# Attention backward on one core: constant matmuls in all four half-steps, the key burst in one, a longer offset, a second value buffer

## Chip, cores, metric

One core of a Trainium2 chip. The metric is the device time of one launch in microseconds (us). Engines: PE (matmul), PEld (its weight loads), DVE (vector), ACT (scalar), POOL (GpSimd), SP (issues most transfers).

## The reference

A gated mix of a 32-head attention block and an S4 convolution, with the gradients of all twelve differentiable inputs. What matters here is attention, forward and backward, for 2048 tokens, 576 channels, heads of 18:

```python
scores = jnp.einsum("bhqd,bhkd->bhqk", q, k) * (Dh ** -0.5)
p = _softmax(scores, axis=-1)
o = jnp.einsum("bhqk,bhkd->bhqd", p, v)
...
_out, _vjp = jax.vjp(_f, A_x, A_wqkv, A_wo, ...)
_grads = _vjp(grad_out)
```

## The kernel before

Heads go in 8 groups of four, 32 rows of the array each; a *unit* is one group with one quarter of the queries (512). A loop over *half-steps* G runs a unit's forward part and, OFF half-steps later, the backward part of an earlier unit. A half-step issues six score rows (32 x 512, of three kinds), then one or two *bursts* that use all 128 rows and 32 columns for each head, then the exps on ACT and the products on DVE. Four half-steps, 16 exps, I call a *quad*; a unit is eight quads. A score row uses 32 rows and 128 columns of the array, a burst's matmuls 128 rows and 32 columns each; going from one shape to the other is a change of *tiling mode*, and the wait that it costs a *drain*.

```python
for nm, src, nb in (("QaT", QaT_d[g], 2), ("KaT", KaT_d[g], 2), ("VaT", VaT_d[g], 1)):
    T[nm] = ga.tile([P, S], BF, tag=nm, bufs=nb, name=nm + "_g")
    nc.sync.dma_start(T[nm], src)
for nm, src, nb in (("Vtok", VaT_d[g], 2), ("Ktok", KaT_d[g], 1), ("Qtok", QaT_d[g], 1)):
    T[nm] = ga.tile([P, NT, 4, HP], BF, tag=nm, bufs=nb, name=nm + "_g")
    nc.sync.dma_start_transpose(out=T[nm].rearrange("p t h w -> p t (h w)"), in_=src)
# ... cut ...
def row(kind, g, b, l, r, j):            # score rows: 4 buffers "S", 2 buffers "dP"
    tg, nb = ("dP", 2) if kind == "P2" else ("S", 4)
    ps = apsp.tile([P, KB], F32, tag=tg, bufs=nb, name="ps_" + kind)
    mm(ps, lhsT=l[r0:r0 + DA], rhs=r[r0:r0 + DA], tile_position=(r0, 0))
# ... cut: in half-step G, G2 = G - OFF, after the six rows ...
if G % 4 == 1 and G2 >= 4:           evs.append(dv_burst(...))      # value burst
if G % 4 == 2 and G2 >= 5:           evs.append(dq_burst(...))      # query burst
if G % 4 in (3, 0) and G2 >= 10:     e_ = dk_half(...)              # key burst, one half each
if G % 4 in (3, 0) and G >= 3:       mm(accO ...)                   # output burst, forward
for (kind, g, b, i, j, ps) in rows:  # ACT: exp of P1 (PT) and P3 (eb); DVE: ds = ps * PT
    ...
for e_ in evs: e_()                  # DVE adds each burst's bank "accB" (one bank) to SBUF
```

PE, ACT, DVE and POOL run in program order; SP's transfers are ordered by the framework's scheduler.

## Time and profile before

| | before |
|---|---|
| median of three runs | 3932.82 us (3932.32 to 3941.81) |
| first exp to last forward exp | 252.1 to 2458.5 us |
| PE, ACT, DVE busy, of the span | 77, 72, 75% |
| mean granted clock, 334 to 2458 us | 0.65 |

The prediction reads the stage in stretches of four microseconds and shows those lines.

### The profile page before, as it was taken

Reading aid. Unit: us, or ns where it says so; the run is one execution under the profiler, and the core shown is the slowest. Engines: PE = TensorE matmul, PEld = TensorE weight load, DVE = VectorE, ACT = ScalarE, POOL = GpSimd, SP = SyncE. Lnnn points to the kernel's source line nnn. Section 1 sums busy time; section 2 is a strip of 40 time slices with the busy share of each in tenths; the row PEclk is TensorE's granted clock in tenths of the full one; section 3 lists DMA queues with packets and bytes.
Section 4 is the critical chain, followed back from the end, with each engine's and each line's share of the span. In section 5 each row is a group of like instructions: output and inputs, shape, how many; then the busy total and the mean of one; then the engine's idle time right before and its main releaser. Section 6 shows DMA issues by size and latency. Waiting matters only on the chain. (4 is left out here: it accounts for less than half of the span.)

```text
span 3930.1 us, 64060 instructions
## 1 busy us (share of the span) xinstructions
PE 3008.7 (77%) x24020; PEld 1073.6 (27%) x24020; DVE 2944.3 (75%) x5131; ACT 2842.5 (72%) x5253; POOL 63.2 (2%) x147
## 2 busy tenths in 40 slices
PE   7969999989999999999999999779344554445421
PEld 2312222222222222222222222135233333333320
DVE  5618878878878878878878878625288888888867
ACT  4549999999989999999999999500266666666610
POOL 0000000000000000000000000100000000000000
PEclk9955666666657666666666666588555555555555
DMA  8535587685686786686776776876456656555456
GB/s 197 166 89 126 128 161 143 133 165 133 138 158 132 138 161 132 138 163 134 142 159 130 135 150 128 184 213 150 69 96 110 110 109 114 103 101 102 85 146 193
DMA packets 1860137, 536.78 MB, mean 137 GB/s; under 512 B 1774991, under 2 KB 1838553, under 8 KB 1859826
## 3 DMA queue, kind: packets, MB, share of 16 engines
q1 hardware_dynamic: 1859826, 532.69, 64.6%
q8 instruction: 189, 3.10, 0.3%
q14 instruction: 122, 1.00, 0.1%
HBM read 99.74 MB, written 60.96 MB: 41 GB/s over the span
## 5 line engine op out<-in xcount | busy, mean ns | idle before, releaser
L602 DVE TENSOR_TENSOR ds<-ps_P,PT 128x512 bf16<-128x512 f32 x2048 | 1360.0, 687 | 353.1 <-PE ps_P L30 226.5
L593 ACT ACTIVATE PT<-ps_P 128x512 bf16<-128x512 f32 x2048 | 1325.6, 652 | 133.6 <-PE ps_P L30 123.3
L597 ACT ACTIVATE eb<-ps_P 128x512 bf16<-128x512 f32 x2048 | 1343.2, 658 | 21.5 <-PE ps_P L30 21.3
L30 PE MATMUL ps_P<-dOaT,VaT_g 32*128 32x512 bf16 x2048 | 1033.6, 530 | 46.9 <-DMA VaT_g<-VaT_d 34.8
L30 PE MATMUL ps_P<-KaT_g,QaT_g 32*128 32x512 bf16 x2048 | 993.4, 520 | 43.9 <-ACT PT L593 4.6
L30 PE MATMUL ps_P<-QaT_g,KaT_g 32*128 32x512 bf16 x2048 | 948.2, 534 | 38.6 <-DMA KaT_g<-KaT_d 6.0
L30 PEld LDWEIGHTS <-KaT_g 32*128 32x128 bf16 x2048 | 150.4, 101 | 647.2 <-issue 632.2
L30 PEld LDWEIGHTS <-VaT_g 32*128 32x128 bf16 x2048 | 192.5, 96 | 419.0 <-issue 373.7
L30 PE MATMUL accO<-PT,Vtok_g 128*32 128x512 bf16 x2048 | 299.9, 568 | 0.0
L30 PE MATMUL accK<-dsT,Qtok_g 128*32 128x256 bf16 x4096 | 285.5, 371 | 5.7 <-DVE dqa L479 3.5
L30 PE MATMUL accQ<-ds,Ktok_g 128*32 128x512 bf16 x2048 | 234.5, 550 | 1.2 <-DVE dvacc L462 0.8
L30 PE MATMUL accV<-eb,dOa 128*32 128x512 bf16 x2048 | 230.3, 541 | 0.6 <-DVE dkacc L503 0.6
L30 PEld LDWEIGHTS <-QaT_g 32*128 32x128 bf16 x2048 | 173.5, 97 | 192.0 <-issue 180.0
L30 PE MATMUL uvp<-RX,E1e 128*128 128x64 bf16 x1152 | 134.2, 290 | 107.8 <-DVE E1e L901 107.8
L30 PE MATMUL tps<-RX,T0w 128*128 128x32 bf16 x576 | 38.4, 233 | 215.5 <-DVE yd L1036 190.5
L882 ACT ACTIVATE kk<-ph,magc 128x512 f32<-128x512 f32 x144 | 91.1, 686 | 147.4 <-DVE E1e L900 112.7
L30 PE MATMUL ph<-thr,lrow 3*128 3x512 bf16 x288 | 124.6, 562 | 88.4 <-ACT ab L875 60.2
L462 DVE TENSOR_TENSOR dvacc<-dvacc,accV 128x512 f32<-128x512 f32 x224 | 153.3, 684 | 26.6 <-PE accV L30 22.3
L479 DVE TENSOR_TENSOR dqa<-dqa,accQ 128x512 f32<-128x512 f32 x224 | 153.1, 684 | 25.1 <-PE accQ L30 22.2
L30 PEld LDWEIGHTS <-E1e 128*128 128x128 bf16 x1152 | 125.3, 124 | 128.9 <-DVE E1e L901 128.3
L30 PE MATMUL ybp<-Rw,E1n 128*128 128x31 bf16 x1152 | 70.0, 233 | 104.2 <-ACT ydi L973 101.5
L887 DVE SCALAR_TENSOR_TENSOR kk<-kk,ph 128x512 f32<-128x512 f32 x144 | 95.1, 682 | 71.6 <-ACT kk L882 71.6
(267 smaller groups left out, 3337.0 us busy)
## 6 DMA issues: line engine op xcount, KB each, us to landing
T0w<-Kp_d SPq DMA_DIRECT2D x36, 512.0 KB
dsT<-ds SPq DMA_TRANSPOSE x512
dqkv_d<-dtk SPq DMA_DIRECT2D x96, 72.0 KB
dqkv_tok<-dqkv_d SPq DMA_DIRECT2D x1, 6912.0 KB
Md_d<-mst SPq DMA_DIRECT2D x144, 36.0 KB
ga_d<-ga_st SPq DMA_DIRECT2D x16, 288.0 KB
dxm_d<-dxm SPq DMA_DIRECT2D x16, 288.0 KB
skw<-Md_d SPq DMA_DIRECT2D x72, 64.0 KB
```

The source lines that it names most:

```text
L30: return nc.tensor.matmul(out, lhsT=lhsT, rhs=rhs, start=start, stop=stop, **kw)
L462: nc.vector.tensor_tensor(a_, a_, acc, op=A.add)
L479: nc.vector.tensor_tensor(U["dqa"], U["dqa"], acc, op=A.add)
L593: nc.scalar.activation(U["PT"][i][:, j, :], ps, ACT.Exp)
L597: nc.scalar.activation(e, ps, ACT.Exp)
L602: nc.vector.tensor_tensor(U["ds"][i][:, j, :], ps, U["PT"][i][:, j, :], op=A.mult)
L882: nc.scalar.activation(B_["kk"][h][:, 4 * q:4 * q + 4, :], ph, ACT.Identity, bias=magc, scale=1.0)
L887: nc.vector.scalar_tensor_tensor(v_, v_, MAGIC, B_["ph"].pop((h, q)), op0=A.subtract, op1=A.subtract)
```

## The change

It adds seven matmuls a quad of an exchange matrix with an identity, whose results nobody reads, to keep the array's clock up; gathers the key burst in one half-step and moves the output bursts to the value and query half-steps, so that one half-step is free for four constants; lengthens the offset by two half-steps (from 37 to 39); gives the value tile a second buffer; and splits the DVE work on a finished unit. Small tiles lose buffers to make room. NFILL holds the number of constants in the value, query, key and empty half-step; the runs below are named by it (const_0004). A constant uses the whole array, a third tiling mode.

```diff
+            NFILL = (1, 1, 1, 4)
-                ptp = ctx.enter_context(tc.tile_pool(name="ptp", bufs=20))
+                ptp = ctx.enter_context(tc.tile_pool(name="ptp", bufs=21))
-                    for nm, src, nb in (... ("VaT", VaT_d[g], 1)):
+                    for nm, src, nb in (... ("VaT", VaT_d[g], 2)):
-                OFF = NST + 5
+                OFF = NST + 7
+                def fill(acc, n, w=4):
+                    o_ = acc[:, (4 - w) * P:4 * P].rearrange("p (a b) -> p a b", b=P)
+                    for _ in range(n):
+                        mm(o_, lhsT=J_bf, rhs=fill_r[:, 0:w, :])
 ... the output burst comes first, then:
+                    if ph in (0, 1, 2):
+                        ACC.append(accB(("accV", "accQ", "accK")[ph]))
+                        fill(ACC[0], NFILL[ph])
+                    elif 0 <= G2 < NTOT:
+                        fill(accB("accF"), NFILL[3])
 ... then value burst (G2 % 4 == 0), query burst (1), whole key burst (2)
 ... post_forward: product, sum and negation of dO move from f1 to f2, one half-step later
 ... one buffer for oT, rl, Ob, dl, dqa; dOa 3 -> 2; eb 12 -> 10
```

## The prediction

> **What bounds the kernel now.** I read the page's busy row and its slices first, then stretches of the attention stage (the only stage the change touches), then two timelines, then the waits.
>
> ```profile
> PE 3008.7 (77%) x24020; PEld 1073.6 (27%) x24020; DVE 2944.3 (75%) x5131; ACT 2842.5 (72%) x5253; POOL 63.2 (2%) x147
> ...
> PE   7969999989999999999999999779344554445421
> ...
> ACT  4549999999989999999999999500266666666610
> ...
> PEclk9955666666657666666666666588555555555555
> ```
>
> Slices 4 to 25 are attention: PE and ACT both read 9, and the granted clock reads only 0.5 to 0.7. A PE that looks full at a low clock may be full only because of it. In stretches of four microseconds:
>
> ```profile
> 412.00:416.00 4.00, 3.56 (x31) 1.07 (x30) 3.67 (x7) 4.00 (x9) 0.00 (x0) 1.00 0.58 131
> 416.00:420.00 4.00, 3.78 (x36) 1.16 (x34) 3.05 (x6) 3.97 (x9) 0.00 (x0) 0.65 0.59 133
> ...
> 476.00:480.00 4.00, 4.00 (x33) 0.86 (x25) 3.05 (x6) 3.76 (x8) 0.00 (x0) 0.50 0.58 131
> 480.00:484.00 4.00, 4.00 (x35) 1.00 (x32) 3.30 (x6) 3.77 (x9) 0.00 (x0) 0.50 0.55 125
> ```
>
> (Columns: stretch, length, busy PE, weight loads, DVE, ACT, POOL, clock, DMA share, GB/s.) At clock 1.00 ACT is busy 4.00 of 4.00 and PE has room. At 0.50 PE is busy 4.00 of 4.00 and ACT is not. The clock alternates, mean 0.65 from 334 to 2458 us. The exps show the pace in the two states, first at full clock, then at half:
>
> ```profile
> 412.75 0.69 ACT L593 ACTIVATE PT<-ps_P 128x512 bf16<-128x512 f32 x1
> 413.23 0.70 ACT L597 ACTIVATE eb<-ps_P 128x512 bf16<-128x512 f32 x1
> 413.70 0.71 ACT L593 ACTIVATE PT<-ps_P 128x512 bf16<-128x512 f32 x1
> ```
>
> ```profile
> 2152.21 0.60 ACT L593 ACTIVATE PT<-ps_P 128x512 bf16<-128x512 f32 x1
> 2152.69 0.62 ACT L597 ACTIVATE eb<-ps_P 128x512 bf16<-128x512 f32 x1
> 2153.38 0.60 ACT L593 ACTIVATE PT<-ps_P 128x512 bf16<-128x512 f32 x1
> ```
>
> At full clock one exp starts every 0.477 us without a break, though a record lasts 0.7 us (records overlap, so starts are counted, not lengths). At half clock each fourth exp comes 0.69 us after the third: it waited for a score row. I call four half-steps a quad: 16 exps. ACT-bound it takes 16 x 0.477 = 7.63 us; at half clock the exps from 2150.55 to 2154.82 give 4.27 us for two half-steps, 8.53 a quad. The waits name one more thing:
>
> ```profile
> ACT PT L593 <- PE ps_P L30: 118.8, 239, 5.7
> ...
> PE ps_P L30 <- DMA VaT_g<-VaT_d: 34.8, 7, 5.7
> ```
>
> Seven group changes, 5 us each, wait for the value tile, which has one buffer.
>
> **What the Trainium skill says.** (1) "TensorE: Matmul & The Clock Gate", Part 1: an activity monitor gives the array half or full clock and decides on free-running windows of about 3.4 us. The trace agrees: in this stage the clock is only 0.5 or 1.0, and changes at multiples of 3.4 us. The page speaks of how busy PE is; here PE is busy 4.00 of 4.00 at clock 0.50 for up to 37.5 us, so busy by records can't be the measure. (2) The same page, "Back-to-back issue gap": N/1.2 ns cold and N/2.4 + 2.5 ns warm, 427 and 216 ns for 512 columns. The trace has 0.40 and 0.23 us between the two groups of four in a value burst. (3) "TensorEngine Tiling (Array Packing)", "Key Properties": a change of tiling mode drains the array. At full clock a burst starts 0.32 us after the last score rows (412.995 to 413.316), 0.1 more than a slot. (4) "ScalarE: Activation LUTs", "What ACT_TABLE_LOAD costs": 186 ns + 0.833 ns per element, 93 ns overlapped, which gives 0.52 us for 512; the trace has 0.477, and I use that.
>
> **Why the clock hunts.** I added up each matmul's rows x columns, as a share of the full array at full rate, in windows laid on the clock's own edges. Half-clock windows followed by half have median 0.343 (middle 90%: 0.274 to 0.380), followed by full 0.371 (0.365 to 0.391). Full-clock windows followed by half have 0.327 (0.261 to 0.368), followed by full 0.415 (0.391 to 0.516). So the switch point, an estimate from these windows, is about 0.37 to 0.39 of the array. The kernel sits on it by its own work: a quad has 24 score rows on a quarter of the array (6 full slots of 512 columns) and four kinds of burst worth 2 slots each, 14 slots of 0.213 us. Over 8.53 us that is 0.35, over 7.63 us 0.39. Once the clock is up ACT holds PE back, and it drops again.
>
> **The change part by part.**
> *Constant matmuls*: one, one, one and four of 128 x 512 in the four half-steps, 7 full slots a quad, some 1,790 in all. Nobody reads them; each is overwritten by a burst's start. Activity becomes 21 x 0.213 = 4.5 us of about 7.8, or 0.57; in the emptiest half-step 4.5 slots of 0.213 in 1.95 us is 0.49. Both clear 0.39. Even from the half clock it is up at once. I expect 1.0 throughout.
> *What they cost*. A score buffer links every other half-step: fourth exp starts, ends 0.62 to 0.67 us later, frees the last row's buffer, row, burst, next half-step's first row, its exp, three more exps. At full clock with 2 burst slots I read 413.863 + 0.385 = 414.248 for the row's end and 414.656 for its exp: slack 0.41 us, some 0.44 if exps end earlier once they don't queue. The new half-steps hold 4, 4, 3 and 4 slots (value + output + 1, query + output + 1, key + 1, 4 alone). Two more cost 0.43, and where constant matmuls stand between column-tiled bursts perhaps two drains of 0.1 each. So three of four half-steps are at or a little over the slack. The worse alternate pair overruns by 0.33 a quad, less 0.14 for the shorter exps. I take 7.8 us a quad: between 7.65 (no drains) and 7.95 (all drains).
> *Value tile doubled*: 34.8 us removed. The query- and key-token tiles still have one buffer and four half-steps (7.8 us) to reload: I leave 2 us a group, 14 us.
> *Key burst whole, output bursts moved*: same matmuls, other places. It leaves an empty half-step for four constants, and gives the query-token tile one half-step more.
> *Split of the dO work*: DVE's chain of six at a unit change (0.26, 0.46, 0.45, 0.46, 0.45, 0.20 us recorded) goes over two half-steps. In the trace it costs a stall ("ACT PT, 0.92 idle" at 2049.96). I leave 0.7 us for each of 31 changes, 22 us.
> *Offset 37 to 39 half-steps*: two more forward-only (1.07 us each), two fewer full ones (in the quad count below), two more in the DVE-bound tail (6.81 us a quad there, 1.7 each): +2.1 and +3.4.
> *Buffers*: 21 probability tiles match the offset; 10 exp tiles and single small tiles are read early enough by my count of half-steps.
>
> **The sum.** Full-mode now: from the first backward row at 292 to the last forward exp at 2458.5, 2166 us for 246.75 quads (8.78 each, all stalls included). After: 246.25 x 7.8 = 1921; ACT's other work, about 118 copies at 0.477, 56; unit changes 22; group changes 14: 2013. Saved 153, less 5.5 for the offset: 147. The stages before 252 and after 2540 us are untouched. 3932.8 - 147 = **3785 us**, 3.8% faster.
>
> **Rivals.** *A: the constants don't count for the clock*, or count by operand values (an exchange matrix and an identity are nearly all zeros). Then the half clock stays and each half-step has up to two slots of 0.427 more: about 2.6 instead of 2.14, or over 400 us slower. For it: I only inferred the measure. Against: rows x columns sort the windows well, and PE's bare busy time does not. *B: PE's order takes ACT's place as the bound.* The constant needs the shared accumulator bank, so it waits for the preceding DVE add before PE can go on. For it: 20.8 us already waited in such adds, and DVE was busy 7.01 of 8 us around 412. Against: by the chain above the add ends near the time the bank is wanted. A stall of 0.3 us a quad makes 3860. *C: pure ACT bound*, all of it hidden: 7.63 a quad, 3743. *D: DMA.* Transposes come 10% closer; share 0.58 in quiet stretches, over 1 at group changes. It could give the 35 us partly back: 3800 to 3815.
>
> **Range and chances.** The pace of 7.65 to 7.95 is 37 us either way; unit and group changes some 25 more. So 3735 to 3855 eight times in ten. Faster by over 2% means under 3854: 0.88. Within 2%, by rival B grown or a clock that still drops sometimes: 0.08. Slower, rival A: 0.04.
>
> **What would show it.** Clock near 1.0 from 334 us to the tail, no 0.50 stretches. ACT busy 97% or more there, exps 0.477 apart in most pairs, first exps late by up to 0.2 us after a half-step with four slots. No wait for the value tile; a small one for key- or query-token tiles. ACT waiting for PE at unit changes only. PE waiting for DVE before a constant would speak for B. A clock that still hunts would sink the whole sum.

## The result

3864.11 us median (3860.61 to 3873.43, 4 runs) against 3933.49 (4 runs); ratio 0.9823, interval 0.9801 to 0.9845. (A ratio is the mean time of one kernel's runs over that of the other's of the same rounds, so not quite the ratio of the medians.) The change wins 1.8%, clear of the noise; I had put down 3.8%. The page after:

```profile
PE 2945.3 (76%) x25828; PEld 1164.4 (30%) x25828; DVE 2914.6 (76%) x5131; ACT 2831.3 (73%) x5253; POOL 63.1 (2%) x146
...
PE   7979999999999989989989999489244545444421
...
ACT  4549999999999989999989998310366666666610
...
PEclk9959999999999999999999999789555555555555
```

1808 more matmuls, PE's busy time a little lower, and the clock row reads 9 through attention. The same stretch of the stage in both kernels, before first (columns: stretch, length, busy PE, PEld, DVE, ACT, POOL, clock, DMA share, GB/s):

```profile
334.00:2340.00 2006.00, 1890.07 (x14696) 492.56 (x14692) 1612.51 (x2679) 1882.56 (x3758) 35.87 (x84) 0.66 0.71 143
```

```profile
334.00:2340.00 2006.00, 1895.48 (x16851) 591.64 (x16853) 1642.07 (x2772) 1935.01 (x3886) 36.50 (x85) 0.98 0.83 147
```

Clock 0.66 to 0.98, as predicted; but in the same time ACT started only 3886 instructions instead of 3758, 3% more. From the first exp to the last forward one the stage takes 2134 us instead of 2206. I took the start of each quad's first exp from the timeline and sorted the units by their place in the group (means from the fifth unit on):

| us | before | after |
|---|---|---|
| clean quad (second half of a plain unit) | 8.0 to 8.6 | 7.98 |
| plain unit (third, fourth place) | 67.9, 68.4 | 65.2, 65.2 |
| first unit of a group forward, last of the old one backward | 70.3 | 67.0 |
| unit in which the backward part changes group | 75.1 | 75.6 |

The last row is the first surprise: at a group change nothing was gained. The waits say why. After:

```profile
PE accK L30 <- DMA Qtok_g<-QaT_d: 26.3, 7, 5.1
...
PE accQ L30 <- DMA Ktok_g<-KaT_d: 12.9, 6, 2.9
```

The wait for the value tile (34.8 us, in the prediction) is gone, and 39.2 us of waits for the token tiles have come, which still have one buffer. The stretches around one such change:

```profile
549.00:557.00 8.00, 7.46 (x70) 2.26 (x67) 6.82 (x13) 7.97 (x17) 0.43 (x1) 1.00 0.63 116
557.00:565.00 8.00, 7.28 (x69) 2.28 (x70) 6.72 (x11) 7.79 (x17) 0.00 (x0) 1.00 1.16 214
565.00:573.00 8.00, 5.50 (x33) 1.41 (x33) 3.46 (x5) 5.66 (x12) 0.43 (x1) 0.75 0.82 211
573.00:581.00 8.00, 8.00 (x63) 1.94 (x64) 4.87 (x8) 5.97 (x12) 0.86 (x2) 0.61 0.92 176
581.00:589.00 8.00, 3.92 (x42) 1.31 (x42) 3.79 (x7) 4.75 (x10) 0.00 (x0) 0.82 0.92 175
```

At 557 the transfers fill up; from 565 PE waits (5.50 of 8), the clock falls, and from 573 PE is busy 8.00 of 8 at 0.61 while ACT does little: after a wait the constants cost double for some microseconds. This is the only kind of place where the clock still falls.

The second surprise is the clean quad. One value half-step after the change, PE:

```profile
448.62 0.37 PE L30 MATMUL ps_P<-KaT_g,QaT_g 32*128 32x512 bf16 x1
448.62 0.38 PE L30 MATMUL ps_P<-dOaT,VaT_g 32*128 32x512 bf16 x1
448.94 0.40 PE L30 MATMUL accO<-PT,Vtok_g 128*32 128x512 bf16 x4
449.27 0.39 PE L30 MATMUL accV<-ident_bf,J_bf 128*128 128x512 bf16 x1
449.59 0.62 PE L30 MATMUL accV<-eb,dOa 128*32 128x512 bf16 x8
450.14 0.38 PE L30 MATMUL ps_P<-QaT_g,KaT_g 32*128 32x512 bf16 x1
```

and ACT over the same time:

```profile
447.90 0.67 ACT L615 ACTIVATE eb<-ps_P 128x512 bf16<-128x512 f32 x1
...
449.82 0.71 ACT L615 ACTIVATE eb<-ps_P 128x512 bf16<-128x512 f32 x1
450.56 0.60 ACT L611 ACTIVATE PT<-ps_P 128x512 bf16<-128x512 f32 x1
...
452.01 0.62 ACT L615 ACTIVATE eb<-ps_P 128x512 bf16<-128x512 f32 x1
```

Output burst to constant, and constant to value burst, are 0.33 and 0.32 us apart where one slot is 0.22: each change of tiling mode costs 0.1. The first row of the next half-step comes at 450.14 and its exp at 450.56; by the 0.477 us between starts it could have begun at 450.30. (The profile shows no idle time, because the record of the exp before lasts to 450.53. The ends tell it: this exp ends 0.63 us after the one before, the others 0.49.) The loop of two half-steps from 447.90 to 452.01 takes 4.11 us, and 3.87 follow in which ACT sets the pace: 7.98.

### The profile page after: what moved, and what is told of

The parts are those of the page before. It is cut to its first block, busy times and chain, and to the rows that moved or that the text cites. A ratio compares the mean times of both kernels' runs of the same rounds, so it can differ in the third digit from the quotient of the medians.

```text
span 3858.9 us, 67450 instructions
## 1 busy us (share of the span) xinstructions
PE 2945.3 (76%) x25828; PEld 1164.4 (30%) x25828; DVE 2914.6 (76%) x5131; ACT 2831.3 (73%) x5253; POOL 63.1 (2%) x146
## 5 line engine op out<-in xcount | busy, mean ns | idle before, releaser
L30 PE MATMUL ps_P<-KaT_g,QaT_g 32*128 32x512 bf16 x2048 | 748.3, 383 | 55.9 <-ACT PT L611 4.4
L30 PE MATMUL ps_P<-dOaT,VaT_g 32*128 32x512 bf16 x2048 | 780.7, 389 | 4.7 <-DMA dOaT<-dOa 4.0
L30 PE MATMUL ps_P<-QaT_g,KaT_g 32*128 32x512 bf16 x2048 | 662.5, 392 | 19.2 <-DMA KaT_g<-KaT_d 5.9
L30 PEld LDWEIGHTS <-J_bf 128*128 128x128 bf16 x1872 | 162.6, 98 | 398.6 <-issue 301.6
L30 PE MATMUL accF<-ident_bf,J_bf 128*128 128x512 bf16 x1040 | 277.6, 391 | 0.0
L30 PEld LDWEIGHTS <-KaT_g 32*128 32x128 bf16 x2048 | 122.0, 93 | 402.3 <-issue 388.7
L30 PE MATMUL accO<-PT,Vtok_g 128*32 128x512 bf16 x2048 | 212.5, 400 | 0.0
L30 PE MATMUL accK<-dsT,Qtok_g 128*32 128x256 bf16 x4096 | 164.0, 282 | 28.6 <-DMA Qtok_g<-QaT_d 26.3
L30 PE MATMUL accQ<-ds,Ktok_g 128*32 128x512 bf16 x2048 | 159.7, 389 | 12.9 <-DMA Ktok_g<-KaT_d 12.9
L30 PE MATMUL accV<-eb,dOa 128*32 128x512 bf16 x2048 | 157.7, 384 | 0.0
```

Of the source, the lines that this page charges most:

```text
L30: return nc.tensor.matmul(out, lhsT=lhsT, rhs=rhs, start=start, stop=stop, **kw)
```

## The experiments

All were correct. Twelve runs; times are medians, ratios to the kernel before.

| label | us | ratio | clock 334 to 2340 | clean quad | group-change unit |
|---|---|---|---|---|---|
| changed kernel | 3864 | 0.982 | 0.98 | 7.98 | 75.6 |
| no_const | 3996 | 1.016 | 0.68 | 8.3 to 9.2 | 75.9 |
| const_0004 | 3852 | 0.979 | 0.95 | 7.84 | 75.4 |
| const_rows32 | 3932 | 0.998 | 0.80 | 7.8 to 8.9 | 76.2 |
| before_const | 3905 | 0.991 | 0.93 | 7.87 | 74.9 |
| const_0013 | 3832 | 0.973 | 0.97 | 7.84 | 73.1 |
| const_first | 3841 | 0.974 | 0.98 | 7.86 | 75.1 |
| value_single | 3858 | 0.981 | 0.98 | 7.98 | 75.8 |
| token_split | 3834 | 0.974 | 0.99 | 7.98 | 71.1 |
| late_load | 3840 | 0.975 | 0.99 | 7.98 | 72.3 |
| together_0013 | 3776 | 0.960 | 0.99 | 7.84 | 66.1 |
| together_1013 | 3811 | 0.969 | 0.99 | 7.98 | 70.2 |
| together_0014 | 3818 | 0.968 | 0.97 | 7.84 | 72.0 |

The first exp starts anywhere from 242.1 to 255.0 us in these kernels, because the stage ahead is scheduled a little differently; differences under some 10 us are therefore read from the quads and units, not from the total.

### Is it the clock?

```diff
-            NFILL = (1, 1, 1, 4)
+            NFILL = (0, 0, 0, 0)
```

> The changed kernel with no constant matmuls at all, everything else kept. Theory (the constants hold the clock, and the clock is what was gained): the clock hunts between 0.5 and 1.0 again, mean about 0.65 in the attention stage, and the time goes back to 3900 to 3950 us. Rival (the gain comes from the moved bursts and the doubled value tile, the constants only fill idle time): within 15 us of the changed kernel's 3864.

Measured: 3996 us, above the range, and the clock hunts:

```profile
334.00:2340.00 2006.00, 1868.91 (x14308) 494.04 (x14310) 1574.40 (x2609) 1831.47 (x3663) 35.87 (x84) 0.68 0.79 139
```

Without constants the rest of the change loses 62 us against the kernel before; the rival, that the constants only fill idle time, falls. A reason fits, though no run isolates it: at half clock the value and query half-steps now hold three slots instead of two, 0.43 us more in a loop of 4.27, and the half-step left empty does not pay that back.

The other way round, constants alone in the kernel before:

```diff
 def dv_burst(...):                 # and dq_burst alike
     acc = accB("accV")
+    fill(acc, 1)
 def dk_half(...):
     if h == 0:
         st["acc"] = accB("accK")
+        fill(st["acc"], 2)
```

> The kernel before with nothing changed but constant matmuls: one ahead of each value and query burst, two ahead of the first half of the key burst. Theory (the clock is all that the change gained): the clock stays near 1.0, clean quads at 7.84 to 7.95, and with the value wait kept and the token waits still hidden by it 3835 to 3865, as fast as the whole change. Rival (the moved bursts and the longer offset are needed to make room): 3880 to 3930.

Measured: 3905 us, in the rival's range, with the clock below the theory's:

```profile
334.00:2340.00 2006.00, 1848.43 (x15787) 524.09 (x15776) 1614.09 (x2711) 1884.29 (x3802) 36.42 (x85) 0.93 0.70 145
```

Its clean quads are 7.87, even better than the changed kernel's. But its plain units take 66.0 and 67.8 us instead of 65.2: the first quad of a unit is 9.9 to 10.2 instead of 8.7, the third 8.9 to 9.6 instead of 8.2, and the clock is lower (0.93). So by the medians of their own rounds constants alone gain 35 us, the rest alone loses 62, and together they gain 69. This is not a clean sum: there are four constants a quad here and seven in the changed kernel. With four, const_0004 below has the rest of the change too and gains 82. So the rest of the change pays only with the clock up; the quads above say that it then makes the unit changes shorter. Which of split, offset and moved bursts does that was not separated.

### What does the clock follow?

```diff
-            NFILL = (1, 1, 1, 4)
+            NFILL = (0, 0, 0, 4)
-                        mm(o_, lhsT=J_bf, rhs=fill_r[:, 0:w, :])
+                        mm(o_, lhsT=J_bf[0:HP], rhs=fill_r[0:HP, 0:w, :], tile_position=(0, 0))
```

> Constants 0, 0, 0, 4 as before, but each on 32 of the array's 128 rows: same time on PE, a quarter of the array. Theory (the clock follows rows x columns): the emptiest stretch has only about 0.34 of the array, under the switch point, so the clock hunts, mean about 0.7, and the time is 3930 to 4000 us. Rival (the clock follows PE's busy time): as with full constants, about 3852, clock 0.95.

Measured: 3932 us, in the theory's range, with a clock of 0.80 (expected: about 0.7). Four constants of full height (const_0004) and four of a quarter's height, the same number of columns:

```profile
334.00:2340.00 2006.00, 1834.24 (x16255) 579.88 (x16254) 1662.66 (x2789) 1926.36 (x3912) 36.73 (x86) 0.95 0.84 148
```

```profile
334.00:2340.00 2006.00, 1873.30 (x15636) 584.21 (x15625) 1605.46 (x2684) 1874.37 (x3766) 36.02 (x84) 0.80 0.81 143
```

PE's busy time is higher in the second and the clock lower. Busy time doesn't hold the clock; the height of the constants does, as rows x columns foretold. (The full-height constants raise the clock although nearly all their values are zero, so dense values aren't needed; no run changed the values alone.) This pair can't tell rows x columns from rows alone. The stored traces can: the attention stage of eight of these kernels (before, after, no_const, before_const, const_rows32, const_0004, const_0013, together_0013), cut into the clock's windows of 3.41 us, gives 4567 of them. One switch point, 0.37 of rows x columns, gives the next window's clock right for 96% of the windows that full clock followed and for 96% of those that half clock followed. The best point of columns alone averages 78% of the two, of rows alone 77%, of PE's busy time 67%.

### What sets the pace at full clock?

```diff
-            NFILL = (1, 1, 1, 4)
+            NFILL = (0, 0, 0, 4)
```

> Four constant matmuls in the empty half-step, none in the other three. Theory (the pace of 7.98 us a quad is the loop through the fourth exp, row, bursts, next row, lengthened by three constant slots and two extra drains in each of two half-steps): the quads fall to 7.63 to 7.70 us if the clock holds, and it should, as the emptiest window still has 0.42 to 0.44 of the array, above the 0.37 to 0.39 read from the kernel before. Some 31 units x 2.6 us = 80 us less than the changed kernel, about 3785. Rival 1 (the clock needs the spread constants): the clock falls now and then, time 3840 to 3900. Rival 2 (the pace is DVE's adds, not PE's bursts): quads stay at 7.98 and the time at 3864.

Measured: 3852 us, quads 7.84. The clock did fall now and then (39 stretches, 201 us, where the changed kernel has 13 and 75), as rival 1 had it, but the clean quads take neither 7.63 nor 7.98. PE was no longer late, so the 7.63 itself had to be wrong. Looking at the records of exps while ACT never waits (here of const_0013; start, length):

```profile
713.40 0.78 ACT L615 ACTIVATE eb<-ps_P 128x512 bf16<-128x512 f32 x1
713.89 0.78 ACT L611 ACTIVATE PT<-ps_P 128x512 bf16<-128x512 f32 x1
...
715.34 0.81 ACT L615 ACTIVATE eb<-ps_P 128x512 bf16<-128x512 f32 x1
715.81 0.82 ACT L611 ACTIVATE PT<-ps_P 128x512 bf16<-128x512 f32 x1
...
721.11 0.92 ACT L615 ACTIVATE eb<-ps_P 128x512 bf16<-128x512 f32 x1
```

Starts are 0.477 apart for most, but the lengths grow, and now and then a start is late. The exp of 721.11 is the sixteenth after that of 713.40: one ends at 714.18, the other at 722.03, 7.85 us later. *Ends* are 0.489 to 0.491 apart all along. ACT can start ahead of its own completion for a while, but 16 x 0.490 = 7.84 is its floor. In the changed kernel's clean quads fifteen ends are 0.488 to 0.492 us apart (medians) and one, behind the value half-step, 0.629: 7.84 + 0.14 = 7.98. The floor was written down before the next run:

```diff
+            NFILL = (0, 0, 1, 3)
```

> Constants 0, 0, 1, 3. Theory: exps complete 0.490 us apart when ACT never waits (their records start 0.477 apart but grow by 13 ns each), so 7.84 us a quad is ACT's floor; and one constant moved from the empty half-step to the key burst's makes all four half-steps equal in array activity, 4.5 slots each. So clean quads at 7.84 as with 0, 0, 0, 4, and fewer drops of the clock than that kernel's 39 windows stretches (200 us at 0.5): 5 to 15 us faster than it, 3837 to 3847. Rival (the 1 costs a drain that shows, or four constants in one place are needed): 3852 or more.

Measured: 3832 us and 7.84; by the trace's clock records there were 27 low stretches (129 us in all) between 334 and 2380 us, where const_0004 had 39 (201 us). The time was better than the range. Of the three ways tried to place four constants a quad (this, const_0004, before_const), four equal half-steps hold the clock best; fewer than four were not tried. Even so it still drops near unit and group changes.

The drains by themselves: the same seven constants, each ahead of the output burst, so that one change of mode less is made in two half-steps.

```diff
+                    if ph in (0, 1, 2): ...fill...     # moved up, before the output burst
                     if G % 4 in (3, 0) and G >= 3:
                         ...output burst...
-                    if ph in (0, 1, 2): ...fill...
```

> The changed kernel, constants 1, 1, 1, 4, with the constant of a half-step issued before the output burst instead of between the output burst and the value or query burst. Same work; one change of tiling mode less in two half-steps (rows, full, columns, rows instead of rows, columns, full, columns, rows). Theory (the pace of 7.98 is the value half-step's loop of 4.11 us plus 3.87 us in which ACT runs alone, and each change of mode is 0.1 us of that loop): quads fall by about 0.1 to 7.86 to 7.90, the time by some 25 us to about 3840. Rival (only the number of slots counts, or the constant now waits for the DVE add ahead of it): quads 7.95 or more, within 8 us of 3864.

Measured: 3841 us, quads 7.86: both as expected. The one late end of a quad comes 0.515 us after the one before instead of 0.629. With two drains gone the seven constants cost almost no pace (7.84 is the floor).

### Where did the value tile's 35 us go?

```diff
-  ("VaT", VaT_d[g], 2)
+  ("VaT", VaT_d[g], 1)
```

> The changed kernel with one buffer for the value tile, as before. Theory (the wait moved: the query- and key-token tiles, with one buffer each, now take the time that the value tile's wait used to hide): value wait of some 5 us x 7 comes back, the token waits of 39 us fall to a few, and the time stays within 12 us of 3864. Rival (the double buffer pays its 35 us and the token waits are something else): 3895 to 3905.

Measured: 3858 us, and the wait is back where it was:

```profile
PE ps_P L30 <- DMA VaT_g<-VaT_d: 46.1, 7, 8.0
```

The token tiles' 39.2 us fall to 3.8 (query 3.8, key none), and the group-change unit takes 75.8 against 75.6. (The 6 us by which the median is better are not the buffer's: the stage starts 7 us earlier and is 2 us longer.) The second buffer bought nothing; it moved the wait to the next tile with one buffer. So, that tile in parts, without more memory:

```diff
-  ("Ktok", KaT_d[g], 1), ("Qtok", QaT_d[g], 1)
+  for nm, src, parts in (("Ktok", KaT_d[g], 2), ("Qtok", QaT_d[g], 4)):   # one tile a part, bufs=1
...
-  lhsT=grp_t[g]["Ktok"][:, i, j, :]
+  lhsT=grp_t[g]["Ktok"][i // (NT // 2)][:, i % (NT // 2), j, :]
-  lhsT=grp_t[g]["Qtok"][:, b * TPQ + qb, j, :]
+  lhsT=grp_t[g]["Qtok"][b][:, qb, j, :]
```

> The changed kernel with the key-token tile in two halves and the query-token tile in four quarters, each reloaded when its own part is done; no more memory. Theory (a group change costs about 12 us because those two tiles can only reload in the last four half-steps, and each wait drops the clock to 0.5 for two windows of 3.4 us): no waits for these tiles, no clock of 0.5 inside the stage, 45 to 70 us less than 3864. Rival (the transfers themselves are the limit at a group change, and another tile takes the wait): within 12 us of 3864.

Measured: 3834 us, 30 less, short of 45 to 70. The token waits are gone, but others come, smaller, and the clock still falls in 6 stretches (41 us between 334 and 2340), where none was expected:

```profile
DVE ds L626 <- DMA dsT<-ds: 14.1, 8, 3.6
...
PE ps_P L30 <- DMA dOaT<-dOa: 8.4, 5, 2.4
```

So the rival had a share: the transfers are crowded there. What may crowd them are tiles for the group *after next* (counted from the group whose backward part ends there), free early and fetched at once:

```diff
 T[nm] = ga.tile([P, S], BF, tag=nm, bufs=nb, name=nm + "_g")    # QaT, KaT, VaT
+if g > 0:
+    nc.gpsimd.memset(T[nm][:, 0:2], 0.0)      # POOL runs in program order: no fetch before this
 nc.sync.dma_start(T[nm], src)
```

> The changed kernel, with the query, key and value tiles of the group after next not fetched before the program reaches that point (GpSimd writes a word of the tile first). Today these 1.5 MB are fetched at the group change, some 60 us early, between the token tiles that are wanted at once. Theory (the token tiles wait in a crowded queue): the key- and query-token waits of 39 us fall to under 20, 15 to 35 us less than 3864. Rival (the waits are set by when the last reader frees the tile): within 10 us of 3864.

Measured: 3840 us, 24 less, with whole token tiles. Their waits fall from 39.2 to 21.0 us, just over the 20 expected, so these fetches were a part of what held the tiles up, not all of it:

```profile
PE accQ L30 <- DMA Ktok_g<-KaT_d: 11.5, 6, 2.9
...
PE accK L30 <- DMA Qtok_g<-QaT_d: 9.5, 7, 1.9
```

### Together

Token tiles split, late fetch, and three choices of constants: 0, 0, 1, 3; then

```diff
-            NFILL = (0, 0, 1, 3)
+            NFILL = (1, 0, 1, 3)      # together_1013
+            NFILL = (0, 0, 1, 4)      # together_0014
```

> Constants 0, 0, 1, 3, token tiles split, tiles of the group after next fetched late. Theory (three separate losses of 32, 30 and 24 us, the last two overlapping because both concern the group change): 3785 to 3805. Rival (all three work on the same wait): 3825 to 3835.

> The same with constants 1, 0, 1, 3. Theory (a score buffer links every other half-step, so the value burst's half-step shares its loop with the key burst's; their sum at 4 and 3 slots with 2 and 1 extra drains is some 7.7 us, still under ACT's 7.84): quads stay at 7.84 and the clock drops less often than with 0, 0, 1, 3, up to 8 us faster than it. Rival (any constant beside the value burst costs its pace): clean quads over 7.9, 5 to 15 us slower than it.

> As together_0013 with four constants in the empty half-step. Theory (the clock still dropped in 16 stretches, 109 us, in together_0013; one more constant lifts the windows that fell short, and four alone cost no pace, as const_0004 kept 7.84): up to 10 us faster, 3766 to 3776. Rival (the drops come at the unit and group changes, not for want of constants): 3774 to 3786.

together_0013 takes 3776 us, ratio 0.9601, interval 0.9578 to 0.9623: it beats both kernels, and my range. ACT is nearly never out of work:

```profile
334.00:2340.00 2006.00, 1875.04 (x16839) 584.97 (x16838) 1758.12 (x2904) 1983.99 (x4031) 38.50 (x106) 0.99 0.88 153
```

together_1013 is a miss of mine: one constant beside the value burst puts the clean quads back to 7.98. I had let the short half-steps of the loop make up for the long one. They can't: after the one late end (0.629 us) ACT is the bound at once, its next ends come 0.488 to 0.490 apart, and what PE delays in one half-step of four is lost. Most of the loss is elsewhere, though: of the 34 us against together_0013, 7 x (70.2 - 66.1) = 29 are in the group-change units (by a profiled run that was 12 us faster than the median). together_0014 is a miss too: quads are 7.84, but the group-change unit takes 72.0 us instead of 66.1, with waits of which together_0013 shows next to nothing (1.7, 1.6 and 0 us):

```profile
DVE ds L628 <- DMA dsT<-ds: 25.5, 11, 3.6
...
PE ps_P L30 <- DMA dOaT<-dOa: 11.0, 7, 2.5
...
PE accK L30 <- DMA dsT<-ds: 10.2, 5, 2.9
```

The clock dropped more often with one constant more, not less: 26 stretches (126 us) up to the last forward exp, 17 of them in group-change units, against 12 (44 us). (The 109 us of the expectation take in 55 us of a stretch that starts at 2374, past the stage's last forward exp at 2301.) Of the 58 us that together_0013 gains over token_split, 7 x (71.1 - 66.1) = 35 are in the group-change units. Why these units differ so much between the three programs stays open; that the scheduler orders SP's transfers differently in them would be a reason, but it was not tested.

## Why the prediction was right or wrong

The direction and the clock's mechanism were right. The sum failed: 3785 expected (3735 to 3855), 3864 measured. All of the miss is in the attention stage: its part from the first backward exp to the last forward exp takes 2091 us where the sum had 2013. The step that failed is the group change; the pace was mis-sized besides.

- **Why the clock hunts, and that constants hold it: right.** Predicted 1.0 throughout, measured 0.98, the rest at group changes. Rows x columns as the measure stood the test of const_rows32. Rival A fell. (Redone from the trace, the four medians of the windows come back within 0.01. The spread of full-clock windows followed by full does not: their middle 90% is 0.336 to 0.431, not 0.391 to 0.516. The best single point is 0.37, the low end of the estimate.)
- **The pace of 7.8 us a quad: its term was mis-sized; it measured 7.98.** 0.18 x 246.25 quads = 44 us of the miss. The floor "16 x 0.477 = 7.63" counted starts; ends count, and the floor is 7.84 (const_0004, const_0013): 0.21 too low, more than the whole 0.18. What PE adds I had put at 0.33 - 0.14 = 0.19; it is 0.14, one late end a quad. The two errors partly cancel, so that the upper end of the range, 7.95, came near 7.98 is luck. The drains that made that end are real (0.1 us each, const_first).
- **Group changes, "2 us a group, 14 us": the step that failed.** The unit of the change takes 75.6 instead of 65.2 us: 10.4 x 7 = 73 us, 59 of the miss. I booked the value tile's 34.8 us as removed although I had seen that the token tiles have one buffer and four half-steps. That is too short for tiles fetched in a crowd: they made PE wait 39.2 us (token_split and late_load each took waits away and gained 30 and 24 us), and the clock falls after such a wait while the constants are in the queue (0.61 from 573 us). Rival D had this with "the 35 us partly back"; all of it came back, and more.
- **ACT's other work and unit changes: 78 us predicted, 57 measured.** From the units: 31 x (65.2 - 8 x 7.98) = 42, and 8 x (67.0 - 65.2) = 14. 21 us the other way. Some of ACT's copies may fall into the time that it waits for PE anyway; this was not traced.
- **The sum**: 44 + 59 - 21 = 82, against a miss of 79. Without the lucky 21 it would have been larger.
- **Rival B** (PE's order takes ACT's place) was half right: PE's order does add to the pace, but by slots and drains. Its evidence was misread: the "20.8 us already waited in such adds" are DVE waiting for PE's burst, not PE for DVE. PE hardly waited for a DVE add before a constant (2.9 and 2.8 us in all); DVE waits for PE more than ever, here ahead of the value add between 334 and 2384 us, before and after:

```profile
DVE dvacc L462 <- PE accV L30: 20.5, 77, 0.3
```

```profile
DVE dvacc L473 <- PE accV L30: 91.6, 183, 0.5
```

- **Rival C** fell: pure ACT bound is not 3743, for its floor was wrong.

## What to carry to other kernels

Measure an engine's floor by the distance of ends where its records overlap, over many instructions, not by starts or by short fast stretches. When a second buffer removes a wait, look for the next tile with one buffer that is reloaded at the same moment: splitting a tile by when its parts fall free needs no memory and can do more than doubling it. Constant matmuls can hold the clock, but they lie on the loop through the next score row: give them to the half-steps with slack, in the order that makes the fewest changes of tiling mode.

## What the Trainium skill lacked or had wrong

- "TensorE: Matmul & The Clock Gate", Part 1 ties the clock to how busy PE is. In const_rows32 PE was busy 1873 of 2006 us at clock 0.80, in const_0004 1834 at 0.95: the array's share counts. A switch point of 0.37 of the array at full rate, an estimate from eight traces, gives the next window's clock right for 96%; PE's busy time at best 67%.
- "TensorEngine Tiling (Array Packing)", "Key Properties" names the drain at a change of mode, but no size: 0.1 us each at full clock here (0.33 and 0.32 us between bursts where a slot is 0.22), and 0.12 us a quad with one less in each of two half-steps (7.98 to 7.86, where ACT's floor of 7.84 hides what more they may save).
- "ScalarE: Activation LUTs", "What ACT_TABLE_LOAD costs" gives, as an estimate from its figures (186 + 0.833 x 512 - 93 ns), 0.52 us a piece for back-to-back activations of 512 elements. Here ends are 0.490 us apart, starts 0.477.
